# Memory's answers as sixteen small products on four banks, and its updates in strips of 32 columns

## The chip, the cores and the metric

The kernel runs on one core of a Trainium2 chip. The metric is the device time of one execution in microseconds (us). The median of three runs of the kernel before is 700.44 us (699.38 to 700.64).

## The reference

A block of a transformer: layer normalisation, then the sum of the input, an attention with a compressive memory, and a gated feed-forward network. There are S = 2048 tokens of D = 448 features, H = 16 heads of 28 features, and N = 4 segments of L = 512 tokens. In the attention, each segment attends to itself causally (`a_dot`) and asks the memory that the segments before it left (`a_mem`):

```python
phi = lambda t: jnp.where(t > 0, t + 1.0, jnp.exp(t))
for s in range(N):
    qs, ks, vs = q[:, :, s], k[:, :, s], v[:, :, s]
    ...
    a_dot = jnp.einsum("bhqk,bhkd->bhqd", p, vs)
    pq = phi(qs)
    num = jnp.einsum("bhld,bhde->bhle", pq, M)
    den = jnp.einsum("bhld,bhd->bhl", pq, z)[..., None] + 1e-6
    a_mem = num / den
    o = g * a_mem + (1.0 - g) * a_dot
    outs.append(o)
    pk = phi(ks)
    M = M + jnp.einsum("bhld,bhle->bhde", pk, vs)
    z = z + jnp.einsum("bhld->bhd", pk)
return o @ wo        # o: the segments put together
```

For each head the memory M is a matrix of 28 x 28 and z a vector of 28. The memory before the first segment is zero. The feed-forward part is `(sigmoid(xn W_gate) * (xn W_up)) W_down` with 1792 inner features.

## The kernel before

The kernel keeps the normalised input transposed in `xs`, one tile per segment (a *block* b = 0..3), split into a high and a low part of fp32r, so that a product of full precision takes eleven matmuls of such parts (`TERMS`).

The *front* (line 272 to 565) goes through the blocks. For each block, `values` multiplies out the values of four tiles of 128 tokens (`pv`, line 330) and stores them in `vst` with 32 columns for each head: 28 values and four ones, so that the sum z comes out as a further column of M. Then seven calls of `keys_queries` (`pp`, line 348) make the keys and queries in chunks of 128 features; the counter of the calls is k. They go to DRAM (`qd`) for the attention, and their phi is kept: that of keys is turned back by `key_rows` (`pk`, line 368) into `kn`, tokens by features, and that of queries goes to DRAM (`fd`, line 361). The next block's `turn` (`pt`, line 99) stands between the calls, and it needs the normalised tile `xn` (`normalise`, line 313, with a copy of its last columns by GpSimd, line 321).

The memory is held for four *groups* of four heads, i = 0..3, 112 = 4 x 28 features each. `update(b, i)` multiplies a group's keys by its values, sixteen heads' pairs at once (112 x 128, over four tiles of tokens), and keeps the four diagonal blocks by a multiplication with the mask `heads`; `mst` is the memory, in two versions in turn, by group. `update` is called at k = 4, 5 and twice at k = 6. `recall(b, i, phi)` multiplies the group's memory by the group's phi of queries (112 rows, 512 tokens), turns the result by 32x32 blocks on DVE (`ts`), divides by the column of z and weighs it (`weigh`, line 126), turns it back (`tb`) and stores it by GpSimd's queue in `od`. Block b's answers are made while block b + 1's values are multiplied (after its tiles t = 1, 2, 3 and after its first key product), and those of the last block between its last key products and the first steps of the feed-forward network. The loads of phi (`phi_queries`, line 385) are issued on SP's queue at the start of the next block, and in the last block at k = 2 to 5.

In the front the order of PE, ACT and DVE is the order of the program (`tc.manual_schedule(engines=FRONT)`). Behind it, the feed-forward network (`gated`, `pgu` line 242 and `pd` line 170), the attention of all segments (`st` line 600, `pa` line 675) and the output projection (`po`, line 756) are put together step by step in an order that is fixed for PE and SP; ACT, DVE and GpSimd are ordered by the planner there.

PSUM has eight banks, given out by tags: `p` and `s` and `gu` two each, `m` and `pd` one each. In the front, `s` serves `pt` (and, in the last block, every second `pp`), `m` and `pd` serve `pk`, `pmm` and `n2`; afterwards `s` serves `st`, `m` serves `pa`, `pd` the down products.

Of the kernel before, what the change touches and what calls it, by code (L numbers as in the profile page):

```python
# [9 lines left out]
F32 = mybir.dt.float32  # L10
F32R = mybir.dt.float32r
AF = mybir.ActivationFunctionType
ALU = mybir.AluOpType
# [3 lines left out]
P = 128  # L17
D = 448
H = 16
DH = 28  # L20
S = 2048
NB = 4
L = 512
NT = 4
F = 1792
NF = F // P
HG = 4
NG = H // HG
GW = HG * DH
# [36 lines left out]
def kernel(  # L66
# [10 lines left out]
    nc = tc.nc  # L77
    V, A, G, T = nc.vector, nc.scalar, nc.gpsimd, nc.tensor
# [33 lines left out]
    def x_block(b):  # L112
        return x[b * L:(b + 1) * L, :].rearrange("(t p) d -> p t d", p=P)
# [5 lines left out]
    def bank(name, tag):  # L119
        return ps.tile([P, L], F32, name=name, tag=tag, bufs=banks[tag])  # L120
# [5 lines left out]
    def weigh(pool, num, g, add):  # L126

        r = pool.tile([P, 16], F32, name="rc", bufs=2)
        n3 = num.rearrange("p (m c) -> p m c", c=32)
        if add:  # L130
            V.tensor_scalar_add(r, n3[:, :, DH], add)
            V.reciprocal(r, r)
        else:
            V.reciprocal(r, n3[:, :, DH])
        V.scalar_tensor_tensor(n3[:, :, :DH], n3[:, :, :DH], g, r.unsqueeze(2).to_broadcast([P, 16, DH]),
                               op0=ALU.mult, op1=ALU.mult)

    qd = [dram.tile([2 * D, 2, L], F32, name=f"qd{b}") for b in range(NB)]
    fd = [dram.tile([D, L], F32, name=f"fd{b}") for b in range(NB)]
# [5 lines left out]
    def eight_k(dtype, name):  # L145
        return mid.tile([P, 8, 256], dtype, name=name, tag="8k")
# [125 lines left out]
    with tc.tile_pool(name="front", bufs=2) as sb, tc.manual_schedule(engines=FRONT):  # L272
        stage = eight_k(F32, "stage").rearrange("p (c a) n -> p c (a n)", c=4)
        vst = eight_k(F32, "vst").rearrange("p (t a) (h c) -> p t (a h) c", t=NT, c=32)
        wv = [late_pair("wv") for _ in range(4)]
        wv = [wv[c // 2][:, c % 2, :] for c in range(8)]
        wqk = {c: sb.tile([P, 8, P], F32R, name=f"wqk{c}", bufs=1) for c in LAST}
        heads = sb.tile([P, P], F32, name="heads", bufs=1)
        mst = [[sb.tile([GW, P], F32, name=f"mst{n}_{i}", bufs=1) for i in range(NG)] for n in range(2)]
        one = sb.tile([P, 1], F32, name="one", bufs=1)  # L280
        kn = eight_k(F32, "kn").rearrange("p (t a) n -> p t (a n)", t=NT)

        def statistics(b, t0, steps):

            stats = sb.tile([P, steps, 6], F32, name=f"stats{steps}")
            mv = sb.tile([P, steps, 2], F32, name=f"mv{steps}")
            vh = sb.tile([P, steps], F32, name=f"vh{steps}")
            for t in range(steps):
                V.bn_stats(stats[:, t, :], acc[b][:, t0 + t, :])  # L289
                V.bn_aggr(mv[:, t, :], stats[:, t, :])  # L290
            V.tensor_scalar(vh, mv[:, :, 1], EPS, -0.5, op0=ALU.add, op1=ALU.mult)
            return mv, vh

        def root(vh):
            y = sb.tile([P, vh.shape[1]], F32, name=f"y{vh.shape[1]}")
            A.activation(y, vh, AF.Sqrt, scale=-2.0)
            return y
# [40 lines left out]
        def values(b, t):  # L338
            pv = bank("pv", "p")
            value_terms(b, t, pv, EARLY[1] if b == 0 else TERMS)  # L340
            store_values(b, t, pv)
# [27 lines left out]
            n = min(P, D - c * P)  # L369
            A.activation(kn[:, :, c * P:c * P + n], pk.rearrange("p (t n) -> p t n", t=NT)[:, :, :n], AF.Copy)  # L370

        def update(b, i):

            pmm = bank("pmm", ("pd", "m")[i % 2])
            for t in range(NT):
                T.matmul(pmm[:GW, :P], kn[:, t, i * GW:(i + 1) * GW], vst[:, t, HG * i:HG * (i + 1), :],  # L376
                         start=t == 0, stop=t == NT - 1)
            if b == 0:
                V.tensor_mul(mst[1][i], pmm[:GW, :P], heads[:GW])
            else:  # L380
                dm = sb.tile([GW, P], F32, name="dm")
                V.tensor_mul(dm, pmm[:GW, :P], heads[:GW])
                V.tensor_add(mst[(b + 1) % 2][i], mst[b % 2][i], dm)

        def phi_queries(b, i):
            phi = sb.tile([GW, L], F32, name="phi", tag="e", bufs=5)
            nc.sync.dma_start(phi, fd[b][i * GW:(i + 1) * GW])
            return phi

        def recall(b, i, phi):  # L390
            ts = sb.tile([P, L], F32, name="ts", bufs=1)
            tb = sb.tile([P, L], F32, name="tb", bufs=2)
            n2 = bank("n2", ("m", "pd")[i % 2])
            T.matmul(n2, mst[b % 2][i], phi, start=True, stop=True)  # L394
            V.transpose(ts, n2)
            weigh(sb, ts, gate[:, i:i + 1], MEM_EPS)
            V.transpose(tb, ts)
            nc.gpsimd.dma_start(od[b][P * i:P * (i + 1)], tb)
# [28 lines left out]
        def split_qk(c):  # L427
            r = raw_qk[c].rearrange("p (c n) -> p c n", c=4)
            A.activation(wqk[c][:, 0:4, :], r, AF.Copy)
            G.tensor_sub(wqk[c][:, 4:8, :], r, wqk[c][:, 0:4, :].bitcast(F32))  # L430
# [39 lines left out]
        for t in range(2):  # L470
# [15 lines left out]
        turn_low(3)  # L486
        split_qk(1)
        split_qk(2)
        G.memset(heads, 1.0)
        h3 = heads.rearrange("p (j c) -> p j c", c=32)  # L490
        G.affine_select(h3, h3, pattern=[[-DH, HG], [0, 32]], base=0, channel_multiplier=1,
                        compare_op=ALU.is_ge, fill=0.0)
        G.affine_select(h3, h3, pattern=[[DH, HG], [0, 32]], base=DH - 1, channel_multiplier=-1,
                        compare_op=ALU.is_ge, fill=0.0)

        ffn = gated()
        for b in range(NB):
            last = b == NB - 1
            phi, xn = {}, {}
            if b > 1:  # L500
                phi = {i: phi_queries(b - 1, i) for i in range(NG)}
            st = None
            for t in range(3 if b == 0 else 0, NT):
                values(b, t)
                if b > 1 and t > 0:
                    recall(b - 1, t - 1, phi[t - 1])
                if b == 0:
                    split_qk(t)
                if last:
                    continue  # L510
                if t == (3 if b == 0 else 0):
                    mv, vh = statistics(b + 1, 0, NT)
                if t == (3 if b == 0 else 0):
                    st = mv, vh, root(vh)
                if t == (3 if b == 0 else 2):
                    A.activation(one, ident[:, 0:1], AF.Exp)
            if st and b > 0:
                st = rstd(*st)
                for n in range(2):
                    xn[n] = normalise(b + 1, n, *st[n])  # L520
            e = {}
            for k, c in enumerate(LAST if last else range(7)):
                e[c] = keys_queries(b, c)
                if b == 0 and c + 4 < 7:
                    split_qk(c + 4)
                if k == 0:
                    if b > 1:
                        recall(b - 1, NG - 1, phi[NG - 1])
                    if b == 0:
                        st = rstd(*st)  # L530
                    if b < 2:
                        nc.sync.dma_start(acc[b + 2], x_block(b + 2))
                    if b == 0:
                        A.activation(gate, gate, AF.Exp, scale=-1.0)
                        V.tensor_scalar_add(gate, gate, 1.0)
                        V.reciprocal(gate, gate)
                        V.tensor_scalar(gate_n, gate, -1.0, 1.0, op0=ALU.mult, op1=ALU.add)
                if last:
                    if k > 0:
                        next(ffn)  # L540
                    if 2 <= k < 6:
                        phi[k - 2] = phi_queries(b, k - 2)
                    if k > 4:
                        begin[k - 5]()
                        recall(b, k - 5, phi[k - 5])
                    continue
                if 2 <= k < 6:
                    key_rows(k - 2, e[k - 2])
                if 4 <= k:
                    update(b, k - 4)  # L550
                if k == 6:
                    update(b, 3)
                n = k - 1 if b == 0 else k + 1
                if 2 <= n < 6:
                    turn(b + 1, n - 2, xn[n - 2])
                if 0 <= n < 4 and n not in xn:
                    xn[n] = normalise(b + 1, n, *st[n])
                if b in (1, 2) and k == 5:
                    next(ffn)
            if last:  # L560
                for i in range(2):
                    for _ in range(FILLS[i]):
                        next(ffn)
                    recall(b, i + 2, phi[i + 2])
                begin[2]()


# [1 line left out]
    sb = ctx.enter_context(tc.tile_pool(name="att", bufs=1, reuse_waits="tile"))  # L569
# [198 lines left out]
    with tc.manual_schedule(engines=MANUAL), ExitStack() as joint:  # L768
        next(steps)
        k = sum(FILLS) + 6  # L770
# [48 lines left out]
```

## Time and profile before

| what | us |
|---|---|
| median of three runs | 700.44 |
| the profiled execution | 699.87 |
| its span, first to last instruction | 698.2 |
| TensorE (PE) busy | 689.2 |
| VectorE (DVE) busy | 569.3 |
| ScalarE (ACT) busy | 344.0 |
| GpSimd (POOL) busy | 144.3 |
| mean granted TensorE clock, share of full | 0.999 |

The prediction's sum is made against the profiled execution. The page names a product by its output tile: `pmm` is an update, `n` an answer (the tile `n2` of the code appears without its number). A matmul of plain fp32 appears as two matmuls in the profile, its two passes, each with its weight load (PEld). In a row of the chain of waits the first number is the start, the second the length, both in us, then the engine, the tile and the line, and how many passes were merged. In a row of a tile's view the durations are in ns, smallest, median and largest.

### The profile page before, as it was taken

The page shows a single profiled execution, that of the slowest core. Times are in us where ns is not written, and L with a number is a line of the kernel's source. Part 1 is how long each engine was busy: PE and PEld are TensorE (multiplying, and loading weights), DVE is VectorE, ACT ScalarE, POOL GpSimd, SP SyncE. Part 2 cuts the span into 40 slices and gives each one's busy share as a digit, 9 for nine tenths or more (in the row PEclk, how much of TensorE's full clock was granted, in tenths as well). Part 3 has the DMA queues.
Part 4 walks back from the last instruction along what each step waited for, and adds up shares of the span by engine and source line. Part 5 has one row for each costly group of instructions (what it writes and reads, how often), then busy time and mean ns, then how long its engine had stood idle before and what let it go on. Part 6 is the DMA issues. An engine that isn't in the chain of part 4 may idle for free.

```text
span 698.2 us, 10430 instructions
## 1 busy us (share of the span) xinstructions
PE 689.2 (99%) x3594; PEld 565.4 (81%) x3594; DVE 569.3 (82%) x994; ACT 344.0 (49%) x563; POOL 144.3 (21%) x349
## 2 busy tenths in 40 slices
PE   8999999999999999999999999999999999999897
PEld 7888878777878787877878778787787878778697
DVE  6665696758789899998998889988898898889864
ACT  4746556343464455544555446455544556444420
POOL 4400010101122232221321223222221232222000
PEclk9999999999999999999999999999999999999999
DMA  7833646597222432143441342324243332315162
GB/s 268 318 129 151 225 184 229 204 321 181 83 68 67 113 98 72 42 113 94 98 114 40 70 123 62 107 55 115 61 104 96 82 70 67 71 44 136 46 209 105
DMA packets 45796, 84.37 MB, mean 121 GB/s; under 512 B 6320, under 2 KB 20400, under 8 KB 45232
## 3 DMA queue, kind: packets, MB, share of 16 engines
q1 hardware_dynamic: 42736, 76.37, 35.3%
q0 software_dynamic: 3008, 7.34, 5.2%
q8 instruction: 28, 0.46, 0.3%
q14 instruction: 24, 0.20, 0.1%
HBM read 51.05 MB, written 32.64 MB: 120 GB/s over the span
## 4 chain that ended last, share of the span: by engine, by line
PE 93%; DVE 3%; DMA 2%; ACT 1%; issue 1%; SPq 0%; POOL 0%; ACTq 0%; DVEq 0%; POOLq 0%
PE pgu L242 41%; PE pd L170 19%; PE pp L348 8%; PE st L600 5%; PE pa L675 5%; PE po L756 5%; PE pv L330 4%; PE pmm L376 2%; PE n L394 1%; DMA qd<-qk 1%; DMA acc<-in_x 1%; PE pt L99 1%; PE pk L368 1%; DVE stats L289 0%; DVE w L654 0%
## 5 line engine op out<-in xcount | busy, mean ns | idle before, releaser
L242 PE MATMUL pgu<-xs,wgu 128*128 128x512 f32 x1232 | 321.0, 398 | 0.0
L242 PEld LDWEIGHTS pgu<-xs,wgu 128*128 128x128 f32 x1232 | 226.1, 188 | 48.2 <-issue 3.0
L170 PE MATMUL pd<-wdn,hh 128*128 128x448 f32 x672 | 161.5, 368 | 0.0
L170 PEld LDWEIGHTS pd<-wdn,hh 128*128 128x128 f32 x672 | 123.2, 188 | 15.6 <-issue 1.0
L615 POOL TENSOR_SCALAR_AFFINE_SELECT w<-w 128x256 f32<-128x256 f32 (+1 forms) x160 | 75.5, 473 | 256.9 <-ACT w L604 213.4
L655 ACT ACTIVATE w<-w 128x1024 f32<-128x1024 f32 (+1 forms) x96 | 86.6, 914 | 74.1 <-DVE w L654 73.4
L604 ACT ACTIVATE w<-st 128x512 f32<-128x512 f32 x128 | 75.4, 590 | 60.2 <-PE st L600 60.0
L654 DVE TENSOR_TENSOR w<-w,mb 128x1024 f32<-128x1024 f32 (+1 forms) x96 | 99.8, 1052 | 0.1
L618 DVE TRANSPOSE_TENSOR_REDUCE mx<-w 128x32 f32<-128x1024 f32 x64 | 79.1, 1236 | 17.1 <-POOL w L615 17.1
L348 PE MATMUL pp<-xs,wqk 128*128 128x512 f32 x308 | 79.0, 405 | 0.0
L173 DVE TENSOR_TENSOR acc<-pd,acc 128x448 f32<-128x448 f32 x112 | 67.6, 603 | 4.6 <-PE pd L170 4.4
L348 PEld LDWEIGHTS pp<-xs,wqk 128*128 128x128 f32 x308 | 56.8, 188 | 14.5 <-issue 2.4
L600 PE MATMUL st<-qk 84*128 84x128 f32 (+3 forms) x256 | 63.9, 310 | 0.0
L250 ACT ACTIVATE sg<-pgu 128x512 f32<-128x512 f32 x56 | 33.3, 595 | 45.7 <-PE pgu L242 45.4
L600 PEld LDWEIGHTS st<-qk 84*128 84x128 f32 x256 | 48.3, 189 | 8.4
L253 ACT ACTIVATE hh<-sg 128x512 fp32r<-128x512 f32 x56 | 35.1, 626 | 38.6 <-DVE sg L252 37.2
L644 DVE STREAM_TRANSPOSE mb<-top 128x1024 f32<-128x1024 f32 x32 | 39.6, 1239 | 10.9 <-POOL top L641 10.5
L355 DVE TENSOR_TENSOR qk<-pp,qk 128x512 fp32r<-128x512 f32 x28 | 19.3, 688 | 31.5 <-ACT e L353 25.7
L330 PE MATMUL pv<-wv,xs 128*128 128x448 f32 x176 | 40.6, 379 | 1.0 <-DVE xs L107 0.8
L257 DVE SCALAR_TENSOR_TENSOR hh<-sg,hh 128x512 fp32r<-128x512 f32 x56 | 38.7, 692 | 1.0 <-ACT hh L253 0.8
L252 DVE SCALAR_TENSOR_TENSOR sg<-sg,pgu 128x512 f32<-128x512 f32 x56 | 37.3, 667 | 2.4 <-PE pgu L242 2.3
L756 PE MATMUL po<-wo,xs 128*128 128x448 f32 x176 | 36.3, 364 | 2.1 <-ACT xs L734 2.1
(100 smaller groups left out, 640.7 us busy)
## 6 DMA issues: line engine op xcount, KB each, us to landing
qk<-qd SPq DMA_DIRECT2D x192, 112.0 KB
qd<-qk SPq DMA_DIRECT2D x28, 512.0 KB
raw<-in_w_ffn SPq DMA_DIRECT2D x14, 512.0 KB
vd<-vst SPq DMA_DIRECT2D x4, 1024.0 KB
vv<-vd SPq DMA_DIRECT2D x16, 256.0 KB
od<-w POOLq DMA_DIRECT2D x16, 256.0 KB, 4.0
ob<-od SPq DMA_DIRECT2D x32, 128.0 KB
out<-acc SPq DMA_DIRECT2D x16, 224.0 KB
```

Of the source, the lines that this page charges most:

```text
L170: T.matmul(pd[:, :D], l, r, start=n == 0, stop=n == len(mms) - 1)
L173: V.tensor_add(acc[b][:, t, :], pd[:, :D], acc[b][:, t, :])
L242: T.matmul(dst, wgu[f][:, w, side * P:(side + 1) * P], xs[b][:, a, :], start=n == 0, stop=n == len(TERMS) - 1)
L330: T.matmul(pv[:, :D], xs[b][:, a, t * P:(t + 1) * P], wv[w], start=n == 0, stop=n == len(TERMS) - 1)
L348: T.matmul(pp, wqk[c][:, w, :], xs[b][:, a, :], start=n == 0, stop=n == len(TERMS) - 1)
L600: T.matmul(st[:, at:at + L - kb * P], self.qk[:KS, 1, h, kb * P:(kb + 1) * P], self.qk[:KS, 0, h, kb * P:], start=True, stop=True)
L604: A.activation(w, st, AF.Copy)
L615: G.affine_select(d, d, pattern=pattern, base=0, channel_multiplier=-1, compare_op=ALU.is_ge, fill=MASK)
L618: V.tensor_reduce(mx[:, 16 * (n - 1):16 * (n + 1)], w3[:, n // 2, :2 * L].rearrange("p (b n) -> p b n", n=32), axis=mybir.AxisListType.X, ...
L654: V.tensor_sub(w, w, m)
L655: A.activation(w, w, AF.Exp, scale=SCALE)
L756: T.matmul(po[:, :D], xs[b][:, a, t * P:(t + 1) * P], out_weights(w), start=m == 0, stop=m == len(TERMS) - 1)
```

## The change

`update(b)` is now one call for all sixteen heads, at k = 6. For each head it multiplies 32 columns of keys (the head's 28, and four of the next head's that nobody reads) by the head's 32 columns of values, over four tiles of tokens; the four heads with the same place j in their groups go to four column strips of PE. The memory `mst` is one tile: head h = 4 i + j lies in rows 32 i and columns 32 j. The mask `heads` is gone, and a memset clears the columns of `kn` behind the last head.

`phi_queries(b, j)` loads, for a place j, the rows of phi of the four heads with that place into four strips of 32 rows. The last j takes two loads, since its last strip ends with the tensor. `recall` makes sixteen products of 28 rows, 32 columns and 512 tokens, each on a 32x32 tile of PE, row strip i and column strip j; group i's four go to one bank, so all four banks (two `s`, `m`, `pd`) are taken at once. The rest of the former `recall` is now `answer(b, i, n2)`, with two buffers of `ts` in place of one.

For blocks 1 and 2 all sixteen products stand after tile t = 2 of the next block's values, with answers 0 and 1 right behind them, answer 2 after t = 3 and answer 3 after the first key product. In the last block the four loads are issued at k = 4, and the products stand after the last key product; answers 0 and 1 are right behind, and answers 2 and 3 after two and four steps of the feed-forward network.

```diff
@@ -275,8 +275,7 @@
-        heads = sb.tile([P, P], F32, name="heads", bufs=1)
-        mst = [[sb.tile([GW, P], F32, name=f"mst{n}_{i}", bufs=1) for i in range(NG)] for n in range(2)]
+        mst = [sb.tile([P, P], F32, name=f"mst{n}", bufs=1) for n in range(2)]
@@ -369,30 +368,41 @@
-        def update(b, i):
-
-            pmm = bank("pmm", ("pd", "m")[i % 2])
-            for t in range(NT):
-                T.matmul(pmm[:GW, :P], kn[:, t, i * GW:(i + 1) * GW], vst[:, t, HG * i:HG * (i + 1), :],
-                         start=t == 0, stop=t == NT - 1)
+        def update(b):
+
+            pmm = bank("pmm", "m")
+            for j in range(HG):
+                for t in range(NT):
+                    for i in range(NG):
+                        h = HG * i + j
+                        T.matmul(pmm[32 * i:32 * i + 32, 32 * j:32 * j + 32], kn[:, t, DH * h:DH * h + 32],
+                                 vst[:, t, h, :], start=t == 0, stop=t == NT - 1)
             if b == 0:
-                V.tensor_mul(mst[1][i], pmm[:GW, :P], heads[:GW])
+                V.tensor_copy(mst[1], pmm[:, :P])
             else:
-                dm = sb.tile([GW, P], F32, name="dm")
-                V.tensor_mul(dm, pmm[:GW, :P], heads[:GW])
-                V.tensor_add(mst[(b + 1) % 2][i], mst[b % 2][i], dm)
-
-        def phi_queries(b, i):
-            phi = sb.tile([GW, L], F32, name="phi", tag="e", bufs=5)
-            nc.sync.dma_start(phi, fd[b][i * GW:(i + 1) * GW])
+                V.tensor_add(mst[(b + 1) % 2], pmm[:, :P], mst[b % 2])
+
+        def phi_queries(b, j):
+            phi = sb.tile([P, L], F32, name="phi", tag="e", bufs=5)
+            rows = fd[b][DH * j:]
+            n = NG if j < HG - 1 else NG - 1
+            nc.sync.dma_start(phi[:32 * n], bass.AP(rows.tensor, rows.offset, [[GW * L, n], [L, 32], [1, L]]))
+            if n < NG:
+                nc.sync.dma_start(phi[32 * n:32 * n + DH], fd[b][D - DH:])
             return phi
 
-        def recall(b, i, phi):
-            ts = sb.tile([P, L], F32, name="ts", bufs=1)
+        def recall(b, phi):
+            n2 = [bank("n2", tag) for tag in ("s", "s", "m", "pd")]
+            for j in range(HG):
+                for i in range(NG):
+                    T.matmul(n2[i][32 * j:32 * j + 32], mst[b % 2][32 * i:32 * i + DH, 32 * j:32 * j + 32],
+                             phi[j][32 * i:32 * i + DH], start=True, stop=True, tile_position=(32 * i, 32 * j))
+            return n2
+
+        def answer(b, i, n2):
+            ts = sb.tile([P, L], F32, name="ts", bufs=2)
             tb = sb.tile([P, L], F32, name="tb", bufs=2)
-            n2 = bank("n2", ("m", "pd")[i % 2])
-            T.matmul(n2, mst[b % 2][i], phi, start=True, stop=True)
-            V.transpose(ts, n2)
+            V.transpose(ts, n2[i])
             weigh(sb, ts, gate[:, i:i + 1], MEM_EPS)
             V.transpose(tb, ts)
             nc.gpsimd.dma_start(od[b][P * i:P * (i + 1)], tb)
@@ -486,24 +496,23 @@
-        G.memset(heads, 1.0)
...
+        G.memset(kn[:, :, D:], 0.0)
...
             if b > 1:
-                phi = {i: phi_queries(b - 1, i) for i in range(NG)}
+                phi = {j: phi_queries(b - 1, j) for j in range(HG)}
             st = None
             for t in range(3 if b == 0 else 0, NT):
                 values(b, t)
-                if b > 1 and t > 0:
-                    recall(b - 1, t - 1, phi[t - 1])
+                if b > 1 and t == 2:
+                    n2 = recall(b - 1, phi)
+                    for i in range(2):
+                        answer(b - 1, i, n2)
+                if b > 1 and t == 3:
+                    answer(b - 1, 2, n2)
@@ -525,7 +534,7 @@
                 if k == 0:
                     if b > 1:
-                        recall(b - 1, NG - 1, phi[NG - 1])
+                        answer(b - 1, 3, n2)
@@ -538,18 +547,15 @@
-                    if 2 <= k < 6:
-                        phi[k - 2] = phi_queries(b, k - 2)
+                    if k == 4:
+                        phi = {j: phi_queries(b, j) for j in range(HG)}
                     if k > 4:
                         begin[k - 5]()
-                        recall(b, k - 5, phi[k - 5])
                     continue
                 if 2 <= k < 6:
                     key_rows(k - 2, e[k - 2])
-                if 4 <= k:
-                    update(b, k - 4)
                 if k == 6:
-                    update(b, 3)
+                    update(b)
@@ -558,10 +564,13 @@
             if last:
+                n2 = recall(b, phi)
+                for i in range(2):
+                    answer(b, i, n2)
                 for i in range(2):
                     for _ in range(FILLS[i]):
                         next(ffn)
-                    recall(b, i + 2, phi[i + 2])
+                    answer(b, i + 2, n2)
                 begin[2]()
```

More of the change, by code (lines that the diff above doesn't have):

```diff
@@ L488 @@
         split_qk(2)
-        G.memset(heads, 1.0)
[L490 to L494, printed above, removed]
+        G.memset(kn[:, :, D:], 0.0)
         ffn = gated()
```

## The prediction

> **What bounds the kernel now.** I read the page's busy times first, then the stretches of the span, then the chain that ended last, and last the single rows of the work that the change touches.
>
> ```profile
> PE 689.2 (99%) x3594; PEld 565.4 (81%) x3594; DVE 569.3 (82%) x994; ACT 344.0 (49%) x563; POOL 144.3 (21%) x349
> 57.00:81.00 24.00, 24.00 (x138) 20.46 (x138) 13.99 (x27) 15.70 (x29) 0.47 (x2) 1.00 0.56 212
> 81.00:118.00 37.00, 37.00 (x194) 30.77 (x193) 30.74 (x69) 21.48 (x39) 3.50 (x8) 1.00 0.54 201
> 118.00:161.00 43.00, 43.00 (x179) 33.35 (x178) 28.22 (x52) 16.10 (x28) 2.70 (x5) 1.00 0.76 260
> 161.00:300.00 139.00, 139.00 (x728) 113.00 (x727) 121.05 (x197) 69.15 (x108) 32.48 (x86) 1.00 0.34 90
> 300.00:640.00 340.00, 340.00 (x1808) 275.81 (x1807) 301.66 (x484) 175.39 (x274) 86.19 (x216) 1.00 0.35 84
> PE pmm L376 <- ACT kn L370: 0.5, 1, 0.5
> ```
>
> In a row of the stretches, PE's busy time stands behind the comma, DVE's third. From 57 to 640 us PE has no idle time, and the last row, PE's waits between 20 and 640 us, has one wait of 0.5 us. So TensorE's own stream is the time: what is taken from it before 161 us, where all memory work lies, comes off the end, unless PE then has to wait. The chain gives the memory's part of the stream:
>
> ```profile
> 75.90 0.76 PE pmm L376 x7
> 76.66 2.56 PE pp L348 x11
> 79.22 1.75 PE pmm L376 x16
> 80.97 4.41 PE pv L330 x22
> 85.38 0.86 PE n L394 x2
> 86.24 2.22 PE pv L330 x11
> 88.46 0.86 PE n L394 x2
> 89.32 2.21 PE pv L330 x11
> 91.53 0.86 PE n L394 x2
> 92.39 2.57 PE pp L348 x11
> 94.96 0.86 PE n L394 x2
> 95.82 2.57 PE pp L348 x11
> 98.39 0.44 PE pt L99 x4
> L376 PE MATMUL pmm<-vst,kn x96: 270/273/363, 36.6 to 117.9; 128*112 128x128 f32 x96
> L394 PE MATMUL n<-phi,mst x24: 590/592/595, 85.2 to 159.9; 112*128 112x512 f32 x24
> ```
>
> Each fp32 product is two passes of PE. An update pass costs 1.75/16 = 0.109 us, an answer (n) pass 0.43 us.
>
> **What is removed.** Updates: 96 passes x 0.109 = 10.5 us. Answers: 24 x 0.43 = 10.3 us. The 0.5 us wait of block 0's first update for kn goes too: the one update now comes after the last key, and kn is long written. Together 21.3 us. DVE loses 12 multiplications and 8 additions for 3 short operations, but is not the bound there (13.99 of 24 us). The mask's GpSimd instructions become a memset of kn's last columns, at the very start, while the inputs load: nothing.
>
> **What is added to PE.** Nothing here uses 32x32 tiles; the nearest rows are those of the attention's pa, four products of 128 rows and 32 columns on four column strips:
>
> ```profile
> 207.65 0.64 PE L675 MATMUL pa<-w,vv 128*32 128x512 f32 x4
> L675 PE MATMUL pa<-w,vv x32: 272/432/617, 207.6 to 209.7; 128*32 128x512 f32 x8, 128*32 128x384 f32 x8, 128*32 128x256 f32 x8, 128*32 128x128 f32 x8
> 207.72 2.29 PE pa L675 x32
> ```
>
> Four passes of up to 0.617 us lie within 0.64 us, so they start about 7 ns apart and run beside each other. All 32 passes take 2.29 us. By the rows above, one after another at 0.43 us per 512 columns, they would need 8 passes each of 0.43, 0.32, 0.21 and 0.11 = 8.6 us; a quarter of it is 2.14, and 0.15 is left for entering and leaving the strips.
>
> *Update:* 64 products, 128 passes, 32 groups of four strips. With 32 columns to stream instead of 128 a group's floor is 0.109/4 = 0.027 us; its issue, four starts 7 ns apart, is the same. Above, the shortest step seen from one pass to the next on a strip is 0.109. Ends: 32 x 0.027 = 0.9 us and 32 x 0.109 = 3.5 us, both plus 0.2. I take 0.035 per group, near the low end because pa's strips really do overlap: 1.3 us, three times 3.9 us.
>
> *Answers:* 16 products on 16 tiles, two passes each. Below, all sixteen side by side: 2 x 0.43 + 16 x 0.007 + 0.2 = 1.2 us. Above, nothing shows that rows overlap as columns do: sixteen products one after another are 16 x 0.86 = 13.8 us. I take 1.2, since the nearest rows overlap fully and each partition feeds four streams there too: three times 3.5 us. [...]
>
> PE's stream: 21.3 - 3.9 - 3.5 = 13.9 us less.
>
> **What is late next.** The order of the front is fixed by hand on PE, DVE and ACT, and the sixteen products come in one piece, so three waits can open.
>
> *The loads of phi.* Each strip load now reads rows of all four head groups, so all of them wait for the block's last store of features.
>
> ```profile
> 81.10 0.34 SPq L356 DMA_DIRECT2D qd<-qk  x1
> 81.76 0.32 SPq L361 DMA_DIRECT2D fd<-e  x1
> 84.67 0.79 SPq L387 DMA_DIRECT2D phi<-fd  x2
> 85.60:87.50 1.90, 1.90 (x9) 1.51 (x8) 1.44 (x5) 0.64 (x2) 0.00 (x0) 1.00 0.74 242
> ```
>
> That store is issued at 81.76, 2.5 us after the last key product (79.22), and the loads that wait for it are issued at 84.67. Counted from the product's end, that is 5.5 us, and 5.0 when no load of phi goes ahead of the store. Five issues of about 0.45 follow; data starts 1 us behind the issue, and 1.0 MB needs 4.1 us at the 242 GB/s of the last row (its stretch holds the ramp; 3 us is the least I allow). Phi's last strip is there after 9.0 to 10.1 us. PE now gets to the answers after 1.3 (update) + 3 x 2.21 (values) = 7.9 us, and would be through them at 9.1; with the last strip's products of 0.9 us behind the landing it is through at 10 to 11. I take 1.5 us of waiting, in block 2 and again in block 3: 3.0 us. On SP, block 3's loads also hold the store of values behind them; nobody needs that before the attention.
>
> *DVE in block 2.*
>
> ```profile
> 97.92 0.70 DVE L395 STREAM_TRANSPOSE ts<-n 128x512 f32<-128x512 f32 x1
> 99.88 0.71 DVE L397 STREAM_TRANSPOSE tb<-ts 128x512 f32<-128x512 f32 x1
> 100.52 0.65 DVE L355 TENSOR_TENSOR qk<-pp,qk 128x512 fp32r<-128x512 f32 x1
> 95.03 0.13 DVE L303 RECIPROCAL y<-y 128x4 f32<-128x4 f32 x1
> 95.87 0.94 DVE L315 TENSOR_SCALAR xn<-acc,mv,y 128x448 f32<-128x448 f32 x2
> 96.52 0.66 POOL L321 COPY xn<-xn 128x64 f32<-128x64 f32 x2 [0.57 <-DVE xn L315]
> ```
>
> An answer is 100.52 - 97.92 = 2.6 us of DVE. Today three of them start 3.1 us apart while PE multiplies values; now answers 0 to 2 start only when all products are done, R, and take 7.8 us in a row. Behind them stand the roots, the normalisation and GpSimd's copy of its tail: the first tile is there 1.8 to 1.9 us later (the first of the two copies ends half of 0.66 us behind 96.52), at R + 9.7. PE wants it after one pv and two pp, 2.21 + 2 x 2.57 = R + 7.35, and can do three of its four transposes, 0.33: 2.0 us of waiting. After it DVE catches up: per key it has about 2.7 us of work (two operations on keys, the low parts, a normalisation) to PE's 3.4 (pp, pt and key rows). Block 1 has no answers, and block 3 no turning: nothing there.
>
> *The last block.* Its phi strips are issued after the fifth key product's store and land about when PE arrives: 0.5 us.
>
> ```profile
> 154.42 0.86 PE n L394 x2
> 155.28 1.87 PE pgu L242 x8
> 158.01 1.63 PE pgu L242 x7
> 160.50 8.63 PE pgu L242 x37
> 169.12 0.24 PE st L600
> ```
>
> The four answers' 10.4 us of DVE start where today the second of them stands (154.42), while PE goes on with these 52 passes of pgu, 12.1 us, which need little of DVE: I put 1 us of waiting on the first st or pd, where the end of the answers and PE meet within 2 us.
>
> **Sum.** 13.9 - 3.0 - 2.0 - 1.5 = 7.4 us less than the profiled execution's 699.87: 692.5. That execution lies 0.57 under the median of 700.44, so the median should come to about 693.
>
> **Rivals.**
> (a) *The waits do not open.* Then 699.87 - 13.9 = 686, 686.5 against the median. For it: phi's landing lies close to PE's arrival. Against: DVE's row order in block 2 is fixed and its 2.0 us do not depend on a DMA.
> (b) *Short passes do not overlap.* The update's groups take 0.109 us each, as the shortest in the rows: 3.7 us per update, 7.2 more in all; but PE then reaches the answers 2.4 us later and the 3.0 us of waiting for phi are gone: about 697. Against it stand pa's starts 7 ns apart. [...]
> (c) *Slower: the row strips do not overlap as the column strips do.* The two passes of a product must follow each other on a tile. In pa the four strips' first passes go together and then the four second ones. If that exchange isn't made for tiles in different rows, each product holds up the next by a pass: 16 x 0.43 + 0.43 = 7.3 us per answer set, 6.1 more three times, 18.3, less the 3.5 us of waiting for phi that this covers: 708. It decides where a set costs more than about 4.7 us: 3 x 3.5 more, less 3.5, is the whole gain. For it: no row here shows a tile of few rows. Against: the sixteen tiles are disjoint and write four banks.
>
> **How the numbers follow.** About 0.2% (1.4 us) is what a measurement of this kernel can tell from no change. My forecast has 0.52 (689.5 to 696), (a) 0.17 (686 to 689.5), (b) 0.18 (696 to 700), (c) 0.13 (above 701, to 720). Faster: 0.52 + 0.17 + most of (b), 0.81. Within 0.2%: the edge of (b), 0.06. Slower: (c), 0.13. The range 687 to 700 leaves out (c) and the lowest of (a); the likeliest case's own is 689.5 to 696.
>
> **What would show it.** Three pieces of about 1.3 us in place of 32 update passes, and three of about 1.2 us (plus waiting) in place of eight answer passes. PE waiting for phi's DMA in blocks 2 and 3. PE waiting at pt for xn in block 2, with three answers in a row on DVE ahead of it. Stretches after 171 us full as before. Wrong makes it an answer set of over 2.5 us, update groups of 0.1 us, or a wait of over 3 us at the first pd or st.

## The result and the profile after

The changed kernel takes 731.52 us, the median of 4 runs (729.69 to 732.21); the kernel before 700.52 us, also of 4 (699.38 to 700.64). The ratio is 1.044, 95% interval 1.0425 to 1.0461: 31 us slower, where 7 us faster was forecast.

Of the changed kernel's page, the busy times and the granted clock in 40 slices; and below them TensorE's waits between 20 and 200 us (in total, times, longest):

```profile
PE 699.8 (96%) x3954; PEld 559.2 (77%) x3954; DVE 564.9 (78%) x977; ACT 343.5 (47%) x563; POOL 144.0 (20%) x347
PEclk9999989697899999999999999999999999999999
PE n L398 <- DMA phi<-fd: 18.3, 12, 4.2
PE pt L99 <- DVE xn L314: 0.8, 1, 0.8
```

PE is busy for 96% of its span instead of 99%. Its clock, full in every slice before, falls in three places (8; 6; 7 and 8), and there is one large wait: the sixteen products (n) wait for the strips of phi, twelve times. That is four strips in each of three sets, so no strip was there in time. The chain that ended last, the same pieces as were shown of before:

```profile
71.95 2.58 PE pp L347 x11
77.06 3.67 DMA fd<-e
82.63 11.35 DMA phi<-fd
94.03 1.97 PE n L398 x7
105.25 0.75 PE pt L99 x4
119.31 2.58 PE pp L347 x11
130.29 11.45 DMA phi<-fd
141.79 2.09 PE n L398 x8
143.88 3.25 PE pv L329 x11
167.74 13.30 DMA phi<-fd
181.09 2.09 PE n L398 x8
183.18 13.90 PE pgu L242 x52
197.08 0.24 PE st L609
```

Each set of answers hangs on a load of phi that lands 11 to 13 us after its issue. The marks against the kernel before, in the two profiled executions: the last key product of block 1 ends at 74.53 (71.95 + 2.58) instead of 79.22, 4.7 us ahead; that of block 2 at 121.89 instead of 118.19 - 1.75 = 116.44, 5.5 us behind; the first st starts at 197.08 instead of 169.12, 28.0 us behind. The span is 727.9 instead of 698.2 us, 29.7 longer. The time is lost in front of the first st, all but 2 us of it.

How the loads ran, in stretches of the changed kernel (PE's busy time behind the comma; clock, share of the 16 DMA engines and GB/s at the end): block 2's loads and the middle of them, the stretches behind the other two sets, and one that was shown of before.

```profile
82.50:94.00 11.50, 4.98 (x25) 0.55 (x24) 0.00 (x0) 2.03 (x3) 0.00 (x0) 0.72 0.24 89
86.00:92.00 6.00, 3.54 (x20) 0.55 (x24) 0.00 (x0) 0.00 (x0) 0.00 (x0) 0.63 0.25 97
143.88:147.10 3.22, 3.22 (x12) 2.95 (x13) 3.05 (x7) 0.00 (x0) 0.38 (x1) 0.73 0.00 0
183.20:190.00 6.80, 6.80 (x23) 5.42 (x24) 6.00 (x12) 1.06 (x2) 1.08 (x2) 0.75 0.82 210
300.00:640.00 340.00, 340.00 (x1809) 275.80 (x1808) 303.41 (x487) 177.59 (x277) 86.96 (x215) 1.00 0.33 82
```

While PE waits and nothing else is under way, the loads move 89 GB/s, and 24% of the DMA engines' time is busy; in the middle of them it is 97 GB/s and 25%, a quarter. 89 GB/s x 11.5 us is 1.02 MB, one whole set of phi. From 300 us on nothing has changed. The strips come in one by one, and the products behind them run slower (PE's rows; in brackets the wait ahead):

```profile
86.25 1.06 PE L398 MATMUL n<-phi,mst 28*32 28x512 f32 x8 [3.69 <-DMA phi<-fd]
88.84 1.93 PE L398 MATMUL n<-phi,mst 28*32 28x512 f32 x8 [1.53 <-DMA phi<-fd]
91.45 1.93 PE L398 MATMUL n<-phi,mst 28*32 28x512 f32 x8 [0.68 <-DMA phi<-fd]
94.03 2.09 PE L398 MATMUL n<-phi,mst 28*32 28x512 f32 x8 [0.64 <-DMA phi<-fd]
```

Right behind the wait of 3.69 us eight passes still take 1.06 us; the next eights take about twice as long, and from 88 to 94 us the granted clock is 0.50.

**The account.** Had phi been there, a set would have been through 1.23 (update) + 3 x 2.21 + 1.2 us after the last key product in blocks 2 and 3, at 83.6 and 131.0 us, and in the last block, where PE runs out of other work at 170.2, at 171.4. They are through at 96.0, 143.9 and 183.2: 12.4, 12.9 and 11.8 us late, together 37.1 us. The work behind them at a lower clock costs 3.25 - 2.21 of pv and 13.90 - 12.13 of pgu, 2.8 us, and block 2's transposes come 2.2 us late. That is 42.1 us of losses. The first st is 28.0 us late, so 14.1 us of stream were saved, against the 13.9 forecast. These 14.1 us are what is left over of the account; the pieces themselves, 21.3 us removed, three updates of 1.23 us and three sets of 1.07 to 1.23 us added (a set whose data is there, from an experiment below), give 14 as well. What the change was forecast to save it saved; three times as much went into the loads and what they hold up.

### The profile page after: what moved, and what is told of

Same layout as the page of the kernel before. It is cut to its first block, busy times and chain, and to the rows that moved or that the text cites. A ratio compares the mean times of both kernels' runs of the same rounds, so it can differ in the third digit from the quotient of the medians.

```text
span 727.9 us, 11130 instructions
## 1 busy us (share of the span) xinstructions
PE 699.8 (96%) x3954; PEld 559.2 (77%) x3954; DVE 564.9 (78%) x977; ACT 343.5 (47%) x563; POOL 144.0 (20%) x347
## 4 chain that ended last, share of the span: by engine, by line
PE 87%; DMA 7%; DVE 4%; SPq 1%; ACT 1%; issue 1%; ACTq 0%; DVEq 0%
PE pgu L242 39%; PE pd L170 18%; PE pp L347 9%; PE st L609 5%; PE po L765 5%; PE pa L684 5%; DMA phi<-fd 5%; PE pv L329 2%; DMA fd<-e 1%; PE n L398 1%; PE pt L99 1%; PE pk L367 1%; SPq L389 1%; DVE xn L314 0%; DMA ob<-od 0%
## 5 line engine op out<-in xcount | busy, mean ns | idle before, releaser
L347 PE MATMUL pp<-xs,wqk 128*128 128x512 f32 x308 | 76.7, 398 | 0.0
L405 DVE STREAM_TRANSPOSE ts<-n 128x512 f32<-128x512 f32 x12 | 8.3, 692 | 44.4 <-PE n L398 44.4
L329 PEld LDWEIGHTS pv<-wv,xs 128*128 128x128 f32 x176 | 33.4, 196 | 8.8 <-issue 3.3
L398 PE MATMUL n<-phi,mst 28*32 28x512 f32 x96 | 22.2, 993 | 18.3 <-DMA phi<-fd 18.3
```

The costliest lines, as they stand in the source:

```text
L329: T.matmul(pv[:, :D], xs[b][:, a, t * P:(t + 1) * P], wv[w], start=n == 0, stop=n == len(TERMS) - 1)
L347: T.matmul(pp, wqk[c][:, w, :], xs[b][:, a, :], start=n == 0, stop=n == len(TERMS) - 1)
```

## The experiments

The code shown of each edit is an excerpt. The theory to be tested, E, an estimate from the share of 0.24 to 0.25 above: a load of phi in the changed kernel has its four strips as the outermost dimension of its access pattern ([[GW * L, n], [L, 32], [1, L]], n = 4 or 3), and such a load runs on as many DMA engines as that dimension has, four of sixteen. Its rival: the loads are slow because there is so little between store and need, whatever their form.

### Sixteen loads of contiguous rows

```diff
-            nc.sync.dma_start(phi[:32 * n], bass.AP(rows.tensor, rows.offset, [[GW * L, n], [L, 32], [1, L]]))
-            if n < NG: ...
+            for i in range(NG):
+                r0 = GW * i + DH * j
+                m = min(32, D - r0)
+                nc.sync.dma_start(phi[32 * i:32 * i + m], fd[b][r0:r0 + m])
```

> The changed kernel, but each place's four strips of phi come by four loads of 32 (or 28) rows instead of one load over four strips, 16 loads per block, in the same place of the order. Theory E (engines): the changed kernel's load counts its four strips outermost, and so only 4 of the 16 DMA engines carry it (DMA share 0.24 while nothing else moves, 89 GB/s). Then the 16 small loads use all engines, and what is left is SP's issue time, 16 x 0.4 = 6.4 us: phi is complete about 13 us after the last key product instead of 19.5; PE waits about 5.5 us in blocks 2 and 3 and 3 in the last: 700 to 708 us. Rival P (place): the loads are late because they all stand behind the block's last store, whatever their shape. Then the time stays at 725 to 735 us.

704.96 us, ratio 1.0057 (1.0040 to 1.0075). 26.6 of the 31 us come back with nothing but the loads' form changed: the same rows, the same tiles, the same order. The time lies in E's range. Of its waits, SP's list and the chain:

```profile
PE n L397 <- DMA phi<-fd: 0.6, 1, 0.6
78.14 8.00 SPq L390 DMA_DIRECT2D phi<-fd  x15
82.62 6.07 PE n L397 x32
```

The long waits are gone. What is left is the issue: fifteen loads take SP's queue 8.0 us, 0.53 each on average, and the products trickle behind them, 6.07 us for the set of block 2. That the small loads use all engines, as was expected, is not shown: from 80.8 to 88.8 us the share was 0.37, at 98 GB/s. Behind the set of block 3 there is also a slow clock, 0.50 from 128 to 134 us, which the last part comes back to.

### Two strips outermost

```diff
+            for i in (0, 2):
+                rows = fd[b][GW * i + DH * j:]
+                n = 2 if i == 0 or j < HG - 1 else 1
+                nc.sync.dma_start(phi[32 * i:32 * (i + n)], bass.AP(rows.tensor, rows.offset, [[GW * L, n], [L, 32], [1, L]]))
```

> The changed kernel with each load of phi cut in two, of two strips each: the same bytes, the same place, eight loads with 2 outermost (the last strips two loads of their own). Theory E (the outermost count is the number of DMA engines, always the same ones): the megabyte moves at about 45 GB/s instead of 89, a DMA share of about 0.12, some 20 us instead of 11.4 after the issue, and the kernel takes 750 to 765 us. Rival (four strips far apart in DRAM are slow for their distance, or a large load is slow by itself): smaller loads are no slower, 725 to 735 us.

One run: 746.3 us, below E's 750 and far above the rival's 735. Two stretches in the middle of block 2's loads, and the wait:

```profile
84.00:88.00 4.00, 0.00 (x0) 0.00 (x0) 0.00 (x0) 0.78 (x2) 0.00 (x0) 0.98 0.13 51
92.00:98.00 6.00, 3.28 (x16) 0.42 (x16) 0.00 (x0) 0.00 (x0) 0.00 (x0) 0.50 0.13 50
PE n L399 <- DMA phi<-fd: 29.4, 12, 10.5
```

Half the outermost dimension gives 50 to 51 GB/s in place of 97, and the wait grows from 18.3 to 29.4 us. The share is 0.13, where two engines of sixteen are 0.125, and 0.25 in the changed kernel, where four are 0.25: the count of E is met in both. The loads here are smaller and more, so that a load is slow for its size or for the distance of its strips is refuted.

### The kernel before with four heads outermost

```diff
-            nc.sync.dma_start(phi, fd[b][i * GW:(i + 1) * GW])
+            nc.sync.dma_start(phi, bass.AP(rows.tensor, rows.offset, [[DH * L, HG], [L, DH], [1, L]]))
```

> The kernel before, where only the load of phi is written with the four heads of a group outermost and 28 rows of each behind, the same bytes to the same places. Theory E: each load then runs on 4 engines and takes about 2.6 us of data instead of 0.95, two at once 5 us, with a DMA share of about 0.25 after 85 us; since the four answers are spread over 10 us, that is nearly hidden: 0 to 2 us slower, 700 to 702.5 us. Rival P: the shape does not matter; the data of the two loads behind the last store still moves within 2 us at about 240 GB/s.

700.49 us, ratio 0.9998 (0.9977 to 1.0019): no effect, and no test. The rows of four neighbouring heads are contiguous, so the pattern is the same 112 rows as before, and from 85.6 to 87.5 us the DMA moved 142 GB/s at a share of 0.40, not the 0.25 of four strips. It says nothing for or against E.

### One load per group, 28 rows outermost

```diff
-        def phi_queries(b, j): ...
+        def phi_queries(b, i):
+            rows = fd[b][GW * i:]
+            nc.sync.dma_start(strips[32 * i:32 * i + DH],
+                              bass.AP(rows.tensor, rows.offset, [[L, DH], [DH * L, HG], [1, L]]))
```

One tile, strips, holds all of phi; four loads fill it. It is paid for by three buffers of e in place of five and one of ts in place of two, so more than the loads differs here.

> The changed kernel, but phi lies in one tile of four places, and one load per head group fills its 28 partitions for all four places (28 rows outermost, then four places): four loads per block, in the same place of the order, of which only the last needs the block's last store. The tile of 8 KB is paid for by three buffers of e instead of five and one of ts instead of two. Theory E: 28 rows outermost spread over 14 engines, phi is complete about when PE arrives, and the sum of the prediction holds without the wait for phi: 688 to 692 us, PE waiting only for xn in block 2 (2 us). Rival W (few partitions): a load that writes only 28 partitions is slow for that; then PE still waits for phi several us per block and the time stays above 705 us.

699.36 us, ratio 0.9983 (0.9960 to 1.0007), between E's range and the rival's: the whole loss comes back, but not the gain. Stretches in and behind block 2's loads, and the chain:

```profile
83.00:84.50 1.50, 0.76 (x4) 0.00 (x0) 0.00 (x0) 1.48 (x2) 0.00 (x0) 1.00 0.86 239
82.70:85.00 2.30, 1.11 (x6) 0.22 (x6) 0.00 (x0) 2.03 (x3) 0.00 (x0) 1.00 0.75 199
85.00:88.00 3.00, 3.00 (x29) 0.47 (x30) 0.12 (x1) 0.00 (x0) 0.00 (x0) 0.69 0.00 0
77.29 4.52 DMA fd<-e
81.82 2.99 DMA strips<-fd
84.95 2.95 PE n L395 x28
```

A load with 28 rows outermost keeps 75% of the engines busy with its start and end, 199 GB/s, and 86% in its middle, 239 GB/s, instead of 24 and 25%. Still the store that it waits for lands only at 81.81, 7 us after the last key product, and phi at 84.81, when PE has been there since 82.7; and behind a wait of 1.2 us, with 1.1 of 2.3 us busy, the clock is 0.69 in the mean, so that the rest of the set takes 2.95 us. This is the forecast's wait for the loads, 1.5 us in each block there and 1.2 and 2.2 here, with the slow clock of 0.69 behind it.

### The same without a store to wait for

```diff
-            rows = fd[b][GW * i:]
+            rows = x[4 * i:]
```

The strips are read from the input x, so the answers are to other data; everything else is as in the last.

> The kernel with a load per group, but the strips are read from the input x instead of the stored features, so no load waits for the block's last store; the memory's answers are therefore those to other data. Theory E': once the loads use enough engines, what the load-per-group kernel still lost (about 15 us against the prediction's stream) is PE's waiting for the stored features (82.6 to 84.9 us and 122 to 126.4 us) and the slow clock that follows such a wait (0.64 to 0.69); without it the three sets of sixteen products cost about 1.1 us each and only the wait for xn (2 to 2.8 us) and a wait in the last block stay: 690 to 693 us. Rival S (the products): sixteen at once hold up PE by themselves, through banks or the change of tiles; then the time stays at 698 to 700 us.

693.25 us, ratio 0.9899 (0.9884 to 0.9915), just above the range of E'. The chain and the waits:

```profile
82.49 1.23 PE n L395 x32
86.70 6.59 DMA od<-tb
121.74 1.07 PE n L395 x32
148.32 1.07 PE n L395 x32
PE pt L99 <- DVE xn L315: 4.4, 1, 4.4
```

With the loads out of the way a set of sixteen products takes 1.07 to 1.23 us. So the loads' lateness, store and all, costs 6.1 us in the kernel with good loads. What remains is the wait for xn, 4.4 us where 2.0 was forecast: the store of the first answer (od<-tb) takes 6.59 us to land, and since tb has two buffers, the third answer's last transposition on DVE waits 2.2 us for it.

### Four buffers for the answers

```diff
-            tb = sb.tile([P, L], F32, name="tb", bufs=2)
+            tb = strips[:, i, :]
```

Made on the last one, so its answers too are to other data.

> As the kernel whose strips come from x (its answers are to other data), but the second transpose of an answer writes into the strips, which are free by then, so that four answers have four buffers in place of two of tb. Theory T: in that kernel PE's wait for xn was 4.4 us instead of the 2.0 of the prediction, because answer 2 waited for the store of answer 0 to land (6.6 us in the chain); with four buffers the wait is 2 to 2.6 us, and the time 690.5 to 691.5 us. Rival: DVE's own work makes the whole 4.4: no change, 693 us.

693.62 us, ratio 0.9910 (0.9889 to 0.9932). The wait for xn falls to 2.3 us in the front, which is the forecast's 2.0, but nothing is gained: the strips are now held by the stores of the answers, and the next loads wait for those, 2.5 us on SP's queue. The part on the wait came true, the part on the time did not.

### The normalisation ahead of the products

```diff
+                if b == 2 and t == 2:
+                    st = rstd(*st)
+                    for n in range(2):
+                        xn[n] = normalise(b + 1, n, *st[n])
```

Made on the load per group; the same lines behind the values are left out in block 2.

> The kernel with a load per group, with block 2's roots and first two normalisations put ahead of the sixteen products instead of behind answers 0 to 2 on DVE. Theory: PE's wait for xn at block 2's first turning (97.55, about 2.6 us) goes, the waits for phi stay: 2 to 3 us less than the load-per-group kernel's 699.4, so 696.5 to 697.5. Rival: DVE is only late elsewhere (the keys' rows come later instead): 699 to 700.

699.76 us, ratio 0.9984 (0.9966 to 1.0001): a miss. PE's wait for xn goes from 2.8 to 1.7 us over the whole run, and the waits for the strips stay, 2.6 us instead of 3.4; between the two kernels no difference can be measured.

### Four products at a time at the old places

```diff
-                if b > 1 and t == 2:
-                    n2 = recall(b - 1, phi) ...
+                if b > 1 and t > 0:
+                    recall(b - 1, t - 1)
```

Loads per group; each group's four products and its answer stand where its one product stood in the kernel before.

> As the kernel with a load per group, but the products are not made sixteen at once: the four products of one head group (one row strip, four column strips) and its answer stand where the group's answer stood in the kernel before, on banks m and pd, and the last block's loads stand where they stood before. So it is the update in strips alone, with answers in the old order. Theory E: updates save 3 x (3.5 - 1.25) + 0.5 = 7.3 us, the answers cost 12 x 1.05 instead of 12 x 0.86, 2.3 us more; no wait for xn: 694 to 697 us. Rival (the wait moves): if the front is held by something else than PE, for example DVE, the saving does not come off the end: 699 to 702 us.

698.06 us, ratio 0.9955 (0.9940 to 0.9969): 1 us above the theory's range and below the rival's. From the chain:

```profile
80.35 0.99 PE n L394 x8
81.34 2.41 PE pv L330 x11
88.14 2.76 PE pp L348 x11
```

There is no wait left in the front. But four small products in place of one cost 0.99 us, and the pv or pp behind them 0.2 more than their 2.21 and 2.57: 1.19 instead of 0.86 us, twelve times, 4 us. By this the updates' gain is kept and the answers' turned into a loss: 7.3 - 4.0 = 3.3 us, of which 2.5 are seen.

### Two groups at a time

```diff
+                if b > 1 and t == 1:
+                    n2 = recall(b - 1, (0, 1))
+                    answer(b - 1, 0, n2)
+                    answer(b - 1, 1, n2)
+                if b > 1 and t == 3:
+                    n2 = recall(b - 1, (2, 3))
+                    answer(b - 1, 2, n2)
```

> As the group-by-group kernel, but two groups' products at a time, eight tiles: groups 0 and 1 after tile t = 1 (whose features are stored one key product earlier), groups 2 and 3 after t = 3; in the last block after the last key product and after two more steps. Theory: a switch to the tiles and back costs PE about 0.33 us and the products of a set 0.86 to 1.06 us whether one, two or four groups go, so six sets cost 8.1 us instead of twelve at 14.3; phi is there in time, DVE has the same order as before: 6 us less than group by group, 691 to 693 us. Rival: the products of different row strips share something (four banks written at once), then eight tiles take 1.9 us and the time stays at 697 to 699.

698.6 us (695.3 to 699.9), ratio 0.9967 (0.9950 to 0.9984): a miss. The eight products take 1.02 to 1.13 us as expected. In the profiled execution, of 696.78 us, PE waits 1.4 us for ACT at an st, 1.1 for the strips and 0.9 for a bank that DVE frees; where the rest up to the median goes is not shown.

### Pairs in block 2, all at once later

```diff
+                if b == 3 and t == 3:
+                    n2 = recall(b - 1, range(NG))
+                    for i in range(3):
+                        answer(b - 1, i, n2)
```

> As the kernel with pairs of groups, but only block 2 keeps the pairs; in block 3 all sixteen products stand after tile t = 3, and in the last block two steps of the feed-forward network later than the last key product. Theory: two sets less, 2 x 1.35 us: 688.5 to 691 us. Rival: DVE's late start on four answers in a row makes PE wait at k = 0 or at the first st and pd: no better than the pairs, 691 to 694.

705.91 us, ratio 1.0075 (1.0050 to 1.0100): a miss, and instructive. Its longest wait:

```profile
PE pp L348 <- DVE ts L402: 6.4, 1, 6.4
```

The products write two banks of the tag s, which the next pp needs; DVE frees the second only after two whole answers, 6.4 us later. Waits of 2.0 and 1.8 us at st follow. That DVE's answers hold up PE is what the rival said, at a higher price.

### Freeing the banks first

```diff
+        def take(n2):
+            for i in range(NG):
+                V.transpose(strips[:, i, :], n2[i])
```

Four transposes in a row free the four banks; the rest of each answer comes later, one by one. Products after the fourth values in block 2, after the first key product in block 3, two steps later in the last block; the normalisation first.

> A version meant to have all gains: a load per group; the sixteen products after tile t = 3 in block 2 and after the first key product in block 3, two steps later in the last block, so that phi has landed; four transposes in a row that free the four banks into the strips; the rest of the answers one by one at later places (block 2: t = 3, k = 0, 3, 4; block 3: k = 0 to 3); block 2's normalisation ahead of them. Theory: no wait is left and the stream is 13.9 us shorter: 685.5 to 688.5 us. Rival: one of the waits moves to the turning or the key rows of block 2 (DVE has 10 us of answers there): 689 to 692 us.

692.13 us, ratio 0.9889 (0.9872 to 0.9906): a gain of 8 us, but 3.6 above the upper end of what was expected and just above the rival's range. In block 3 the products wait 1.6 us for a bank that pp holds; two stretches there and the chain:

```profile
121.30:124.00 2.70, 1.11 (x17) 0.20 (x32) 1.35 (x2) 1.72 (x3) 0.00 (x0) 1.00 0.58 235
124.00:126.50 2.50, 2.50 (x33) 1.26 (x25) 1.36 (x3) 0.00 (x0) 0.00 (x0) 0.65 0.96 314
125.13 4.16 PE pp L348 x11
```

One stall of 1.6 us, and behind it the clock is 0.65 in the mean of the stretch and the next pp takes 4.16 us instead of 2.57: as much again.

### Block 3's products one key later

```diff
-                        if b == 3:
-                            take(recall(b - 1, phi))
-                            answer(b - 1, 0)
...
+                    if k == 1:
+                        take(recall(b - 1, phi))
+                        answer(b - 1, 0)
+                        answer(b - 1, 1)
```

> As the last version, but block 3's sixteen products stand after the second key product instead of the first. Theory: there PE waited 2.7 us (121.2 to 123.9) because one of the four banks, an s, still held the first key product that DVE had to read, and the next key product then took 4.16 us instead of 2.57 at a granted clock of 0.65; one product later the bank is free: 3.5 to 4.5 us less, 687.5 to 689 us. Rival: the wait is for the strips' loads and remains, or moves to the next s: 691 to 693 us.

690.71 us, ratio 0.9852 (0.9824 to 0.9880), against 700.79 before: 10 us faster than the kernel before and 41 faster than the changed one, though 1.7 above the upper end of what was expected. The two last versions are not told apart for certain, since their intervals overlap. The stretch with the products, and the chain:

```profile
124.00:130.00 6.00, 5.08 (x36) 3.60 (x21) 5.54 (x11) 1.70 (x4) 0.00 (x0) 1.00 0.69 232
126.39 2.83 PE pp L348 x11
158.49 0.23 PE st L620
```

A wait of 0.9 us is left, for a bank that DVE frees. The clock stays full, and pp takes 2.83 us. The first st is at 158.49 instead of 169.12: 10.6 us ahead, and the whole run keeps nearly all of it.

## Why the prediction was wrong, point by point

**The step that failed** is "1.0 MB needs 4.1 us at the 242 GB/s of the last row", with its conclusion "I take 1.5 us of waiting, in block 2 and again in block 3: 3.0 us". The 242 GB/s were those of loads of another form; the changed kernel's move 89, and the 1.0 MB takes 11.5 us. From the first issue, at 80.80 on SP's queue in the changed kernel, to the landing at 93.98 (82.63 + 11.35) it is 13.2 us:

```profile
80.80 2.59 SPq L389 DMA_DIRECT2D phi<-fd  x4
```

The forecast took the rate of a queue from one access pattern to another without asking what the pattern does to it. Phi's last strip was forecast 9.0 to 10.1 us after the last key product; it came after 93.98 - 74.53 = 19.5. The whole term for phi was 3.0 + 0.5 us; measured it is 37.1, the slow clock within the sets included. That is the wrong sign of the result by itself. The sixteen loads, same rows in another form, took back 26.6 us, which shows the form to be the cause; the two strips outermost made it worse. No view here lists the engines, but their busy share where only the loads move data gives an estimate of the count: 0.13 for two outermost, 0.25 for four and 0.86 for 28 rows are 2.1, 4.0 and 13.8 of sixteen. The 14 expected for 28 rows was the author's estimate, which no run before it had shown.

**The time before the issue** was off too, by little: the forecast has 5.0 us from the last key product to the first load when none goes ahead; it was 80.80 - 74.53 = 6.3.

**A term that was missing** is the clock. The forecast counted waits as their own length. Here the work behind a wait can run slower as well: 2.8 us behind the second and third set, and in the experiments means of 0.69 and 0.65 over some 3 us behind waits of 1.2 and 1.6 us. In half-microsecond stretches the clock of the load-per-group kernel is 1.00 up to 86.0 us and 0.50 from 86.5 to 89.5, so such a mean is a mixture of the two. How long the wait was does not decide alone whether the clock falls. With the sixteen loads, the set of block 2 trickled for 6.07 us and the clock stayed full, but behind the set of block 3, where the longest wait was 0.6 us, it was 0.50; with the normalisation ahead it fell in the last block, where the set's longest wait was 0.27 us. Waits of 1.4 us (for st, with pairs) and of 1.3 us (for the strips, block 3 with the normalisation ahead) left it at 1.00. Two stretches of the sixteen loads, blocks 2 and 3, and one of the normalisation ahead:

```profile
82.00:88.70 6.70, 6.70 (x37) 1.93 (x35) 1.58 (x4) 2.03 (x3) 0.00 (x0) 1.00 0.40 106
128.00:134.00 6.00, 6.00 (x17) 4.13 (x14) 5.24 (x11) 0.19 (x1) 1.27 (x3) 0.50 0.23 87
152.00:155.00 3.00, 3.00 (x30) 1.15 (x10) 1.06 (x4) 0.00 (x0) 0.00 (x0) 0.50 0.99 338
```

What sets the slow clock off these runs leave open.

**What held.** The products, from the changed kernel's own groups (count, then shortest, median and longest pass in ns) and its chain:

```profile
L378 PE MATMUL pmm<-vst,kn x384: 196/196/217, 42.4 to 122.9; 128*32 128x32 f32 x192
42.45 1.23 PE pmm L378 x86
```

- *Update.* 128 passes in 1.23 us, 1.3 forecast. Each lasts 196 ns and they start under 10 ns apart, so rival (b), passes that don't overlap, is refuted, and its price of 0.109 us per group with it.
- *Answers.* 1.07 to 1.23 us for a set whose data is there, 1.2 forecast. Rows overlap as columns do, and rival (c) is refuted, though the time came out on its side and above it.
- *The stream.* 14.1 us saved by the account above, 13.9 forecast.
- *DVE in block 2.* The pp behind the transposes starts at 105.25 + 0.75 = 106.0, R + 10.0 with R = 96.0, where R + 7.8 would be without a wait: 2.2 us late, 2.0 forecast. DVE sets that time, as forecast; of the 2.2 us TensorE itself waits only 0.8, since the slow clock, 0.85 in the mean from 96 to 102 us, makes it late too. That the wait grows to 4.4 us, for want of a third tb, when the first answer's store takes 6.59 us to land (2.3 to 3.3 in the changed kernel) was not in the forecast.
- *The last block.* 1 us of waiting was forecast at the first st or pd; where the loads do not hold up the products (strips from x) a pd waits 0.5 us for DVE.
- *Rival (a)*, 686.5 us, asks that no wait opens. The best version, with the same products, is at 690.71: 10 of the 14 us are there once the loads, the banks and the row order are seen to.

**The chances.** 0.13 stood on slower, all of it for a mechanism that was refuted. A rival "the loads run at a fraction of the rate" was absent, though the only bounds given for them, 3 and 4.1 us, came from rows of another access pattern.

## What to carry to other kernels

When a change gives a load a new access pattern, its rate is a new unknown. Look at which dimension is outermost, and put many rows there: here the share of the sixteen DMA engines was 0.13 with two strips outermost, 0.25 with four and 0.86 with 28 rows. Where several small products replace large ones, their cost on TensorE was right to 0.1 us here; what decided was when their data and banks were there, so first put them where both have slack. A stall of TensorE can cost as much again in a slow clock behind it (1.6 us for one of 1.6 here), though not every one does, so look for it in the trace.

## What the runs showed of the hardware

- Loads with two 32-row strips outermost ran at 50 to 51 GB/s and a share of 0.13, with four at 97 GB/s and 0.25, with 28 rows outermost and the four strips inside at 239 GB/s and 0.86, each in the middle of the loads.
- Sixteen fp32 products on sixteen 32x32 tiles, two passes each, take 1.07 us together; one alone of the large ones takes 0.86. Eight of them take 1.02 to 1.13 us, and four 0.99 with 0.2 more on the next products, so four save nothing against one large one.
- TensorE's clock was 0.65 to 0.69 in the mean of some 3 us behind waits of 1.2 to 1.6 us, and 0.50 for 6 us with no wait over 0.6 us ahead; waits of 1.3 and 1.4 us elsewhere left it at 1.00.
- Issuing fifteen loads of 64 KB or a little less took SP's queue 8.0 us, four loads of 192 to 256 KB 2.59; the DMA rate was 98 GB/s from 80.8 to 88.8 us with the small ones, and 89 from 82.5 to 94 us with the large.
